# A new instruction order for the first 28 slices, on eight PSUM banks, with fillers that read a constant

## The chip, the core and the metric

The kernel runs on one core of one Trainium2 chip. The metric is the device time of one launch in microseconds (us). Times of single instructions come from one profiled execution of the kernel.

## The reference

A cross attention between a sequence and a small state, in both directions, feeds a gated feed-forward layer. For each of 8 batches and 8 heads, `x` has 512 rows and `state` has 32 rows, of 64 numbers each.

```python
scores  = scale * x @ state^T;   a  = softmax(scores);   xread = a @ state      # 512 rows per head
scores2 = scale * state @ x^T;   a2 = softmax(scores2);  sread = a2 @ x         # 32 rows per head
x = concat([xread, sread], axis=2).transpose(0, 2, 1, 3).reshape(B * S, H * D)  # (8 * 544) x 512
gate = maximum(x @ w_gate, 0);   val = x @ w_val         # d_model 512 -> d_ff 1536
return (gate * val) @ w_out                              # back to 512
```

## The kernel before

The kernel never forms `xread`. For a batch b it multiplies the state by the two weight matrices first (`U = state @ w`, per head), and then the normalised attention by `U`. All products are bf16 with float32 sums.

The work of one batch: transpose `x` on TensorE (`x_T`, `x_T2`, lines 169 to 186), or by a DMA in later batches; scores (`att_sc`, L200); exponential on ScalarE (`att_exp`, L207); row sums and reciprocals on VectorE (`att_sum`, L213 and L215); scaling (`att_scale`, L219) on VectorE or on GpSimd; transposing the attention (`att_T`, L235, copied out by `att_out`, L249). The state block is converted to bf16 (`state_conv`, L121 and L124), transposed (`state_T`, L129) and copied out (`state_out`, L133). `U` is made in units: `c_unit` covers a few columns of both weight matrices, `u_unit` covers 512 columns of one; both issue small tiled products in `u_mm` (L291), into two banks, one for each half of the heads, and are copied out by `c_out` (L311) and `u_out` (L301).

A slice (b, jf) is 128 of the 1536 hidden columns for the 512 rows of batch b: `gv` (L316) makes gate and value in four products of 512 columns into two banks, `relu` (L340) copies the gate out on ScalarE, and `mult` (L344) multiplies on VectorE. Three `o` steps of four products (`out_part`, L353) make an output tile of 128 rows, and `fin_x` (L361) copies it out and stores it. The state's own read (`sr_mm`, L264, with the bf16 copy `xa` of x that `x_pad`, L256, makes on GpSimd) is normalised on VectorE by a reciprocal and a scale (`sr_norm`, L271 and L273), which read the `sr` bank.

Every engine runs its instructions in the order in which the kernel issues them. The order has two parts. The first is a string, `program`: each word is a step. `gv.0.5@41` is slice (0, 5) with its two products in banks 4 and 1; `co.0.128.128.1.act` copies half 1 of a `c` unit out on ScalarE; `nx` is `att_scale`, `nr` is `att_sum`, `ex` is `att_exp`, `xc` converts x, `xo` copies its transposes out, `ao` is `att_out`, `sto` copies the state's transposes out, `stc` is `state_conv`, `xp` is `x_pad`, `sr` and `sn` are the state's read and its normalisation, `dw` loads a block of columns of one weight matrix, `dx`, `ds`, `do` and `df` are other loads. All of those loads are issued by GpSimd, in the order of the string. The string covers 28 slices: batches 0 and 1, and four slices of batch 2. The second part is a loop, which starts at slice (2, 4) and hands out banks by turns, beginning with banks 0 and 1:

```python
    def bank(name, kind="r"):
        if given:
            n = given.pop(0)
        ...
            n = turn["r"] % 6 if kind == "r" else 6 + turn["o"] % 2
```

In the string of before, banks 0 to 5 hold everything but the output tiles, which use 6 and 7. Bank 7 is also the target of the fillers. A filler (`spin`, L432) is a product of 128x512 whose result nobody reads. It reads `warm`, a piece of a buffer that is filled much later and which VectorE sets to zero first (L396). There are 23 fillers, all among the first steps.

Of the kernel before, what the change touches and what calls it, by code (L numbers as in the profile page):

```python
# [9 lines left out]
BF16 = mybir.dt.bfloat16  # L10
# [6 lines left out]
def kernel(  # L17
# [9 lines left out]
    nc = tc.nc  # L27
# [42 lines left out]
    stT = const.tile([128, B, NJ, 64], BF16, name="stT")  # L70
    br = const.tile([128, NJ, B, Ns], BF16, name="br")
    hs_sb = const.tile([128, NF, B * Ns], BF16, name="hs_sb")
    warm = hs_sb.rearrange("p f n -> p (f n)")[:, 0:512]
    tiny = const.tile([128, 1], FP32, name="tiny")

    xf, xb, xT, e_sn, a_sn, ANS, U, hsb, sr_sb = {}, {}, {}, {}, {}, {}, {}, {}, {}
# [316 lines left out]


    ctx.enter_context(tc.manual_schedule())
    nc.vector.memset(warm, 0.0)  # L396
    xf[0] = xin.tile([128, H, NC, D], FP32, name="xf", tag="xf")
    for eng, j in ((nc.sync, 0), (nc.scalar, None), (nc.scalar, 1)):
        if j is None:
# [28 lines left out]
    warm_ps = psum.tile([128, 512], FP32, name="warm_ps", tag="b7")  # L428

    def spin(n, cols=512):  # L430
        for i in range(n):
            nc.tensor.matmul(warm_ps[:, 0:cols], warm[:, 0:128], warm[:, 0:cols], start=True, stop=True)  # L432

    steps = {"spin": spin, "stc": state_conv, "stT": state_T, "sto": state_out, "xc": x_conv_pair, "xT": x_T, "xT2": x_T2, "xo2": x_out2, "on": lambda: nc.gpsimd.memset(xa[:, :, :, D:D + 1], 1.0), "dw": w_load, "dx": x_load, "ds": lambda: state_dma(nc.gpsimd, 2, B), "do": wo_dma,
             "df": lambda b: x_dma(b, (nc.gpsimd,)), "xo": x_out,
             "sc": att_sc, "ex": att_exp, "nr": att_sum, "nx": att_scale, "aT2": att_T2, "ao2": att_out2, "aT": att_T, "ao": att_out,
             "c": c_unit, "co": c_out, "u": u_unit, "uo": u_out, "gv": gv, "re": relu, "mu": mult, "o": out_part,
             "of": fin_x, "xn": x_next, "xp": x_pad, "sr": sr_mm, "sn": sr_norm}  # L440
    program = """
    dx.1.0.2 dx.1.1.2 stc.0.0.act stc.0.1.dve spin.7 stT.0@0 xc.0.0.dve dw.0.0.128 sto.0.act dw.1.0.128 on xc.0.1.dve
    spin.3 xT.0.1@1 dw.0.128.128 xT.0.0@2 xo.0.1.dve xo.0.0.act dw.1.128.128 spin.3 sc.0.0@3 dw.0.256.256 ex.0.0
    spin.1 xT.0.2@4 xT.0.3@5 xo.0.2.dve dw.1.256.256 xo.0.3.act nr.0.0 spin.3 sc.0.1@0 dw.0.512.256 xT2.1.0@1 ex.0.1
    nx.0.0 xo2.1.0.act nr.0.1 dw.1.512.256 spin.2 xT2.1.1@2 xo2.1.1.act sc.1.0@3 dw.0.768.256 nx.0.1 ex.1.0
    dw.1.768.256 spin.2 c.1.0.128@45 c.0.0.128@01 co.1.0.128.0.dve aT.0.1@2 co.0.0.128.0.act aT.0.0@3 co.1.0.128.1.dve
    co.0.0.128.1.act dw.0.1024.256 sc.1.1@4 ao.0.1.dve ao.0.0.act nr.1.0 ex.1.1 dw.1.1024.256 spin.2 c.0.128.128@05
    gv.0.0@12 co.0.128.128.1.act nr.1.1 co.0.128.128.0.act nx.1.0.pool re.0.0 gv.0.1@34 mu.0.0 re.0.1 nx.1.1.pool
    c.1.128.128@50 mu.0.1 co.1.128.128.1.act c.0.256.256@12 co.1.128.128.0.act c.1.256.256@30 dw.0.1280.256
    co.0.256.256.0.dve co.0.256.256.1.act aT.1.1@5 aT.1.0@4 co.1.256.256.0.act co.1.256.256.1.dve dw.1.1280.256  # L450
    gv.0.3@21 ao.1.1.act ao.1.0.dve dx.2.0.1 re.0.3 gv.0.2@30 mu.0.3 ds re.0.2 c.1.512.256@54 mu.0.2 gv.1.2@21
    co.1.512.256.1.act co.1.512.256.0.act do.0.6 c.0.512.256@30 re.1.2 gv.1.5@45 co.0.512.256.0.dve xp.1
    co.0.512.256.1.act mu.1.2 re.1.5 gv.1.3@23 mu.1.5 re.1.3 gv.1.1@04 do.6.12 mu.1.3 re.1.1 c.1.768.256@15 xp.0
    mu.1.1 gv.1.4@23 co.1.768.256.0.act co.1.768.256.1.act c.0.768.256@04 re.1.4 gv.1.0@15 co.0.768.256.0.dve
    co.0.768.256.1.act df.3 mu.1.4 re.1.0 gv.1.6@20 mu.1.0 re.1.6 gv.0.4@41 mu.1.6 re.0.4 gv.0.6@35 mu.0.4 re.0.6
    gv.1.7@20 mu.0.6 re.1.7 c.0.1024.256@41 c.0.1280.256@35 mu.1.7 co.0.1024.256.0.act xT2.2.0@2 stc.1.0.pool
    co.0.1024.256.1.act co.0.1280.256.1.dve xT2.2.1@0 stc.1.1.pool co.0.1280.256.0.act xo2.2.0.dve gv.0.5@41
    stc.3.0.pool stc.3.1.pool xo2.2.1.dve re.0.5 stc.2.1.pool gv.0.10@53 stc.2.0.pool mu.0.5 re.0.10 stT.1@2 gv.0.9@40
    mu.0.10 sto.1.act re.0.9 sc.2.1@1 gv.0.8@52 ex.2.1 mu.0.9 re.0.8 nr.2.1 gv.0.11@34 re.0.11 mu.0.8 gv.0.7@10
    nx.2.1.pool mu.0.11 re.0.7 sc.2.0@5 o.0.0@6 mu.0.7 ex.2.0 nr.2.0 c.1.1280.256@32 c.1.1024.256@14  # L460
    co.1.1280.256.1.act u.2.1.1024@50 o.0.1 co.1.1024.256.0.dve co.1.1024.256.1.act nx.2.0.pool uo.2.1.1024.1.dve
    uo.2.1.1024.0.act o.0.2 co.1.1280.256.0.act u.2.0.0@21 xn.3 of.0.0.dve u.2.1.0@45 uo.2.0.0.1.act u.2.1.512@03
    uo.2.1.0.0.dve o.0.3@7 uo.2.1.0.1.act uo.2.0.0.0.dve uo.2.1.512.0.act aT.2.0@1 aT.2.1@4 uo.2.1.512.1.dve
    ao.2.0.act o.0.4 ao.2.1.act o.0.5 gv.2.1@50 of.0.1.act re.2.1 gv.1.10@23 mu.2.1 re.1.10 gv.1.11@14 mu.1.10 re.1.11
    gv.2.3@50 mu.1.11 re.2.3 gv.2.2@23 mu.2.3 re.2.2 u.2.0.1024@14 u.2.0.512@50 mu.2.2 uo.2.0.1024.1.act sr.0@2
    o.0.6@6 uo.2.0.512.1.act uo.2.0.512.0.dve sn.0 gv.1.9@34 uo.2.0.1024.0.dve re.1.9 gv.1.8@05 mu.1.9 re.1.8
    gv.2.0@21 mu.1.8 re.2.0 o.0.7 mu.2.0 o.0.8 o.0.9@7 of.0.2.dve sr.1@3 sn.1 xp.2 xp.3
    """
    for word in program.split():
        word, _, banks = word.partition("@")  # L470
# [107 lines left out]
```

The softmax here doesn't subtract the row's maximum and nothing guards it: scores larger than these inputs give would overflow.

## Time and profile before

| | us |
|---|---|
| median of 4 runs | 225.6 |
| the 4 runs | 224.38, 225.58, 225.62, 225.64 |
| the profiled execution, whole | 225.11 |
| its span, first to last instruction | 223.3 |
| TensorE busy in it | 215.6 (97%) |
| first slice starts in it | 14.22 |
| the loop's first slice, (2, 4), starts in it | 56.72 |

The span is what the trace covers, so positions in the trace count from its first instruction, and 1.8 us of the profiled execution lie around it. A timeline line gives start, length, engine, source line, output and inputs, shapes and count; in square brackets stands the idle time of the engine before it and what ended that. "PE" is TensorE's products, "PEld" its weight loads.

The loads that GpSimd issues land one after the other. In this execution: the rest of batch 0 at 6.62 us, batch 1 at 8.46 and 9.77, the weight blocks from 10.49 to 26.64, batch 2 at 29.28, the rest of the state at 30.29, the two halves of the output weights at 34.0 and 37.83, and batch 3 at 40.74.

### The profile page before, as it was taken

The page shows a single profiled execution, that of the slowest core. Times are in us where ns is not written, and L with a number is a line of the kernel's source. Part 1 is how long each engine was busy: PE and PEld are TensorE (multiplying, and loading weights), DVE is VectorE, ACT ScalarE, POOL GpSimd, SP SyncE. Part 2 cuts the span into 40 slices and gives each one's busy share as a digit, 9 for nine tenths or more (in the row PEclk, how much of TensorE's full clock was granted, in tenths as well). Part 3 has the DMA queues.
Part 4 walks back from the last instruction along what each step waited for, and adds up shares of the span by engine and source line. Part 5 has one row for each costly group of instructions (what it writes and reads, how often), then busy time and mean ns, then how long its engine had stood idle before and what let it go on. Part 6 is the DMA issues. An engine that isn't in the chain of part 4 may idle for free.

```text
span 223.3 us, 4840 instructions
## 1 busy us (share of the span) xinstructions
PE 215.6 (97%) x1937; PEld 106.5 (48%) x1967; DVE 128.5 (58%) x226; ACT 124.8 (56%) x236; POOL 53.3 (24%) x58
## 2 busy tenths in 40 slices
PE   7999999999999999999999999999999999999994
PEld 3544455444544444444444444445444445666543
DVE  3587888666595648664877468646875433222100
ACT  4599877874467645675566456645655444222221
POOL 8889756503301525006000700000000000000000
PEclk9999999999999999999999999999999999999999
DMA  7999999160147671781159113511311111111132
GB/s 153 180 195 196 207 233 285 41 169 3 47 101 231 117 262 56 165 253 51 48 128 277 56 57 92 100 50 47 94 50 47 48 47 50 48 68 73 52 94 94
DMA packets 37799, 25.48 MB, mean 114 GB/s; under 512 B 18864, under 2 KB 33200, under 8 KB 37776
## 3 DMA queue, kind: packets, MB, share of 16 engines
q1 hardware_dynamic: 24912, 16.85, 26.6%
q0 software_dynamic: 11968, 7.47, 21.6%
q10 hardware_dynamic: 896, 0.85, 1.4%
q8 instruction: 15, 0.25, 0.4%
q14 instruction: 8, 0.07, 0.1%
HBM read 18.35 MB, written 8.91 MB: 122 GB/s over the span
## 4 chain that ended last, share of the span: by engine, by line
PE 95%; issue 2%; ACT 1%; DVE 0%; DVEq 0%
PE o_ps L353 38%; PE gv_ps L316 37%; PE gv_ps L333 5%; PE up L291 4%; PE warm_ps L432 3%; PE sc_ps L200 2%; PE upc L291 1%; PE sr_ps L264 1%; PE o_ps L379 1%; ACT U L311 1%; PE aT_ps L235 1%; PE xT_ps L186 1%; PE stT_ps L129 0%; ACT xT L189 0%; PE xT_ps L169 0%
## 5 line engine op out<-in xcount | busy, mean ns | idle before, releaser
L316 PE MATMUL gv_ps<-ans,U 128*128 128x512 bf16 x373 | 93.9, 379 | 0.5
L353 PE MATMUL o_ps<-wo_sb,h_sb 128*128 128x512 bf16 x357 | 91.6, 379 | 2.1 <-issue 1.9
L344 DVE TENSOR_TENSOR h_sb<-gv_ps,g_sb 128x512 bf16<-128x512 f32 x96 | 65.4, 689 | 43.8 <-ACT g_sb L340 42.6
L340 ACT ACTIVATE g_sb<-gv_ps 128x512 bf16<-128x512 f32 (+1 forms) x108 | 62.7, 580 | 49.2 <-PE gv_ps L316 34.5
L316 PEld LDWEIGHTS <-U 128*128 128x128 bf16 x384 | 35.8, 98 | 40.4 <-issue 0.6
L353 PEld LDWEIGHTS <-h_sb 128*128 128x128 bf16 x372 | 35.2, 98 | 39.8 <-issue 1.7
L361 ACT COPY o_sb<-o_ps 128x512 f32<-128x512 f32 x29 | 17.1, 590 | 16.5 <-PE o_ps L353 16.5
L301 ACT CAST U<-up 128x512 bf16<-128x512 f32 x36 | 18.9, 594 | 11.4 <-PE up L291 11.4
L301 DVE CAST U<-up 128x512 bf16<-128x512 f32 x36 | 22.8, 684 | 2.2 <-PE up L291 1.9
L142 POOL CAST xb<-xf 128x1024 bf16<-128x1024 f32 x10 | 10.6, 1088 | 52.6 <-DMA xf<-in_x_dram 45.7
L256 POOL COPY xa<-xb 128x2048 bf16<-128x2048 bf16 (+1 forms) x9 | 15.3, 1709 | 12.5 <-issue 7.6
L213 DVE TENSOR_REDUCE cs<-e_sn 128x16 f32<-128x512 bf16 x16 | 10.9, 684 | 7.9 <-ACT e_sn L207 7.9
L344 DVE TENSOR_TENSOR hs_sb<-gv_ps,g_sb 128x256 bf16<-128x256 f32 x12 | 5.1, 425 | 15.3 <-PE gv_ps L333 10.5
L207 ACT ACTIVATE e_sn<-sc_ps 128x512 bf16<-128x512 f32 x16 | 9.6, 599 | 5.6 <-PE sc_ps L200 5.5
L291 PEld LDWEIGHTS <-stT 64*32 64x32 bf16 x512 | 5.7, 89 | 11.3 <-issue 10.1
L311 ACT CAST U<-upc 128x512 bf16<-128x512 f32 (+1 forms) x20 | 9.5, 533 | 1.4 <-PE upc L291 1.3
L432 PE MATMUL warm_ps<-hs_sb 128*128 128x512 bf16 x20 | 7.8, 504 | 1.4 <-DVE hs_sb L396 1.2
L219 DVE TENSOR_TENSOR a_sn<-e_sn,rc 128x512 bf16<-128x512 bf16 x12 | 8.3, 692 | 0.6
L200 PEld LDWEIGHTS <-xT 128*128 128x128 bf16 x128 | 5.7, 98 | 3.8 <-ACT xT L177 0.7
L291 PE MATMUL up<-wg_sb,stT 64*32 64x512 bf16 x144 | 7.4, 382 | 0.0
L333 PE MATMUL gv_ps<-br,wg_sb 128*128 128x256 bf16 x48 | 7.2, 273 | 0.1
L333 PE MATMUL gv_ps<-br,wv_sb 128*128 128x256 bf16 x48 | 7.2, 273 | 0.0
(64 smaller groups left out, 130.3 us busy)
## 6 DMA issues: line engine op xcount, KB each, us to landing
out_dram<-o_sb SPq DMA_DIRECT2D x31, 256.0 KB, 2.3
xf<-in_x_dram SPq DMA_DIRECT2D x4, 1024.0 KB, 6.3
wo_sb<-in_moe_w_out_dram POOLq DMA_DIRECT2D x2, 768.0 KB, 14.4
wg_sb<-in_moe_w_gate_dram POOLq DMA_DIRECT2D x5, 256.0 KB, 8.6
wv_sb<-in_moe_w_val_dram POOLq DMA_DIRECT2D x5, 256.0 KB, 9.2
xf<-in_x_dram POOLq DMA_DIRECT2D x1, 1024.0 KB, 15.1
xb<-in_x_dram POOLq DMA_DIRECT2D x3, 256.0 KB, 6.1
xb<-in_x_dram POOLq DMA_DIRECT2D x1, 512.0 KB, 11.1
```

Source lines behind the costliest of these rows:

```text
L213: nc.vector.reduce_sum(out=cs, in_=e_v, axis=AX.X)
L256: nc.gpsimd.tensor_copy(out=v[:, hs:hs + src.shape[1]], in_=src)
L291: nc.tensor.matmul(dst[parity][32 * j:32 * j + 32], stT[r:r + 64, b, j, 32 * parity:32 * parity + 32], wsb[r:r + 64, j, lo:lo + n], start= ...
L301: copy[eng](out=U[b][:, w, kc, lo:lo + 512], in_=held["u", b, w, lo][kc])
L311: copy[eng](out=U[b][:, :, kc, lo:lo + n], in_=held["c", b, lo][kc])
L316: nc.tensor.matmul(ps[w], U[b][:, w, kc, f0:f0 + 128], ANS[b][:, kc].rearrange("p c t -> p (c t)"), start=(kc == 0), stop=(kc == NK - 1))
L333: nc.tensor.matmul(ps[w][:, 0:nt], wsb[:, j, f0:f0 + 128], br[:, j].rearrange("p b n -> p (b n)"), start=(j == 0), stop=(j == NJ - 1))
L340: nc.scalar.activation(out=g_sb[:, 0:n], in_=ps[0][:, 0:n], func=AF.Relu)
L344: nc.vector.tensor_tensor(out=dst, in0=ps[1][:, 0:n], in1=held["g", b, jf][:, 0:n], op=ALU.mult)
L353: nc.tensor.matmul(held["o", b, tsub], src[:, jf, tsub * 128:(tsub + 1) * 128], wo_sb[:, jf], start=(jf == 0), stop=(jf == NF - 1))
L361: copy[eng](out=o_sb, in_=held["o", b, tsub])
L432: nc.tensor.matmul(warm_ps[:, 0:cols], warm[:, 0:128], warm[:, 0:cols], start=True, stop=True)
```

## The change

The order of the string is new, and so are the banks in it. Banks 6 and 7 now also hold slices, units and scores. There are 16 fillers in place of 23; they read a built-in constant of ones, one column wide, spread over 128 and 512 columns, and the memset is gone. Some steps change their engine: the scaling `nx` of batches 1 and 2 moves from GpSimd to VectorE, the first half conversion `xc.0.0` from VectorE to ScalarE, and several copies change between ScalarE and VectorE. Units of `U` for neighbouring columns stand next to each other more often, and the state reads `sr.0` and `sr.1` stand together at the end, in banks 2 and 0. The loop is unchanged.

```diff
-    warm = hs_sb.rearrange("p f n -> p (f n)")[:, 0:512]
...
-    nc.vector.memset(warm, 0.0)
+    one = nc.const_aps.tensor(1.0, (128, 1), BF16)
...
-            nc.tensor.matmul(warm_ps[:, 0:cols], warm[:, 0:128], warm[:, 0:cols], start=True, stop=True)
+            nc.tensor.matmul(warm_ps[:, 0:cols], one.to_broadcast([128, 128]), one.to_broadcast([128, cols]), start=True, stop=True)
...
-    dx.1.0.2 dx.1.1.2 stc.0.0.act stc.0.1.dve spin.7 stT.0@0 xc.0.0.dve dw.0.0.128 sto.0.act dw.1.0.128 on xc.0.1.dve
-    spin.3 xT.0.1@1 dw.0.128.128 xT.0.0@2 xo.0.1.dve xo.0.0.act dw.1.128.128 spin.3 sc.0.0@3 dw.0.256.256 ex.0.0
-    spin.1 xT.0.2@4 xT.0.3@5 xo.0.2.dve dw.1.256.256 xo.0.3.act nr.0.0 spin.3 sc.0.1@0 dw.0.512.256 xT2.1.0@1 ex.0.1
...
-    gv.0.0@12 co.0.128.128.1.act nr.1.1 co.0.128.128.0.act nx.1.0.pool re.0.0 gv.0.1@34 mu.0.0 re.0.1 nx.1.1.pool
-    c.1.128.128@50 mu.0.1 co.1.128.128.1.act c.0.256.256@12 co.1.128.128.0.act c.1.256.256@30 dw.0.1280.256
...
-    o.0.6@6 uo.2.0.512.1.act uo.2.0.512.0.act sn.0 gv.1.9@34 uo.2.0.1024.0.dve re.1.9 gv.1.8@05 mu.1.9 re.1.8
-    gv.2.0@21 mu.1.8 re.2.0 o.0.7 mu.2.0 o.0.8 o.0.9@7 of.0.2.dve sr.1@3 sn.1 xp.2 xp.3
+    dx.1.0.2 dx.1.1.2 stc.0.0.act stc.0.1.dve xc.0.0.act dw.0.0.128 spin.7 stT.0@0 xT.0.0@1 xc.0.1.dve dw.1.0.128 on
+    sto.0.dve xT.0.1@2 xo.0.0.dve dw.0.128.128 xo.0.1.act dw.1.128.128 dw.0.256.256 spin.4 xT.0.3@3 dw.1.256.256
+    xT.0.2@4 xo.0.3.dve sc.0.0@5 xo.0.2.act ex.0.0 sc.0.1@6 dw.0.512.256 xT2.1.0@0 ex.0.1 nr.0.0 xo2.1.0.act
...
+    co.0.0.128.0.dve aT.0.0@2 co.0.0.128.1.act ao.0.1.dve dw.1.1024.256 ao.0.0.act spin.1 c.1.128.128@43 nr.1.1
+    c.0.128.128@56 co.1.128.128.1.act gv.0.0@01 co.0.128.128.0.act nr.1.0 co.0.128.128.1.act dw.0.1280.256 re.0.0
+    gv.0.1@23 co.1.128.128.0.act nx.1.1 re.0.1 nx.1.0 dw.1.1280.256 c.0.256.256@57 c.1.256.256@60 co.0.256.256.1.act
+    co.0.256.256.0.dve aT.1.0@4 aT.1.1@2 co.1.256.256.0.act ao.1.0.dve gv.0.2@75 dx.2.0.1 ao.1.1.dve
...
+    c.1.1024.256@57 xo2.2.0.act stc.3.0.pool gv.1.10@10 co.1.768.256.0.dve stc.2.0.pool co.1.768.256.1.dve
+    co.1.1024.256.1.act stc.2.1.pool stT.1@4 gv.1.11@23 stc.3.1.pool re.1.10 sto.1.dve co.1.1024.256.0.act mu.1.10
...
+    mu.2.0 gv.2.2@34 of.0.1.act re.2.2 gv.1.6@20 mu.2.2 re.1.6 o.0.6@6 mu.1.6 o.0.7 o.0.8 gv.2.1@15 of.0.2.dve re.2.1
+    gv.2.3@34 mu.2.1 re.2.3 o.0.9@7 mu.2.3 sr.0@2 sr.1@0 sn.0 sn.1 xp.2 xp.3
```

## The prediction

> **What bounds the kernel now.** I read the page's shares first, then the chain that ended last. TensorE is busy for 97% of the span and carries 95% of the chain, the other engines 58% at most:
>
> ```profile
> PE 215.6 (97%) x1937; PEld 106.5 (48%) x1967; DVE 128.5 (58%) x226; ACT 124.8 (56%) x236; POOL 53.3 (24%) x58
> ...
> PE 95%; issue 2%; ACT 1%; DVE 0%; DVEq 0%
> ```
>
> A busy share hides waits, because a matmul's end is modelled. So I went on to the chain in order of time:
>
> ```profile
> 11.44 1.01 ACT xT L189
> ...
> 45.04 4.32 PE gv_ps L316 x20
> ```
>
> The last line is 20 products of 512 columns in 4.32 us, 0.216 us each. That is the price of a product in a dense stretch, so a `gv` slice or an `o` step (four products) costs 0.864. By start times, TensorE is dense from the first `gv` (14.22 us) to the end: only the weight and U groups cost more than their products. Before 14.22 it runs fillers and waits on a chain of transposes, copies (the first line is one on ScalarE), exponentials and sums. The hand-written program ends where slice (2,4) of the loop begins, at 56.72 us; the 166.6 us from there to the end of the span have the same instructions in both kernels. So the question is when slice (2,4) starts.
>
> Two views give the clocks of that stretch. The timeline of TensorE's head:
>
> ```profile
> 1.18 3.17 PE L432 MATMUL warm_ps<-hs_sb 128*128 128x512 bf16 x7 [1.18 <-DVE hs_sb L396]
> ...
> 5.84 0.96 PE L169 MATMUL xT_ps<-id,xb 128*128 128x128 bf16 x8
> 6.64 0.81 PE L432 MATMUL warm_ps<-hs_sb 128*128 128x512 bf16 x3
> ```
>
> The first seven fillers start 0.427 apart, those from 6.64 on 0.216 apart; within the eight transposes the spacing falls from 0.107 to 0.056 at about 6.5 us. And the timeline around the end of the program and of GpSimd's state work:
>
> ```profile
> 30.38 5.43 POOL L124 TENSOR_SCALAR st_b<-st_f,odd 128x256 bf16<-128x256 f32 x6 [3.87 <-DMA st_f<-in_state_dram]
> ```
> ```profile
> 56.35 0.43 PE L264 MATMUL sr_ps<-xa,e_sn 128*32 128x65 bf16 x32
> ...
> 56.72 1.04 PE L316 MATMUL gv_ps<-ans,U 128*128 128x512 bf16 x3
> 56.85 0.17 DVE L271 RECIPROCAL rr<-sr_ps 128x2 f32<-128x2 f32 x1 [0.56 <-PE sr_ps L264]
> ...
> 57.06 0.29 DVE L273 TENSOR_TENSOR sn<-sr_ps,rr 128x128 bf16<-128x128 f32 x1
> ```
>
> GpSimd waits 3.87 us for the state load, then needs 0.91 us for each of six conversions. TensorE goes on to `gv` straight after `sr`, while VectorE still reads the `sr` bank until 57.35.
>
> **Fillers.** 16 instead of 23. The memset (0.27 us, L396) and TensorE's wait for it go, so the first filler starts at about 0.8 instead of 1.18. This gains nothing: the seven end at 3.8, and `stT.0` needs `st_b`, whose VectorE half ends at 4.01 as before (the state block lands at 3.4). I cost the new operand at nothing: it is a product of the same 128x512 shape, and a few tenths more would still end before 4.1.
>
> **Head.** I followed each engine by hand with the rows' durations (ScalarE: copies and exponentials of 512 0.6, of 1024 1.01; VectorE: sum and reciprocal 0.96, scale 0.69, copies of 512 0.42 to 0.69). `xc.0.0` moves to ScalarE (done 4.55), so the first transposes start at 4.65 instead of 5.84. The rest of x0 lands at 6.62 and is transposed next, so both scores can run early: exp 0.0 ends at 8.7 (8.52 before), exp 0.1 at 9.3 (10.36 before). The halves of x1 land at 8.46 and 9.77 on the same queue; the second half's transposes start at 9.9 instead of 10.76, and its copy ends at 11.6 instead of 12.45. ScalarE then has exp 1.0, a cast, exp 1.1, a cast and `ao.0.0`, which ends at 13.7. `gv.0.0`: **13.76** against 14.22, 0.46 earlier.
>
> **Dense part, work.** Both have 28 `gv` and 10 `o` steps: 38 x 0.864 = 32.83. A `c` or `u` unit costs 0.217 and entering and leaving such a group about 0.22: one unit alone took 0.437 (19.47 to 19.90), two 0.653, three 0.866. Before has 17 units in 9 groups behind `gv.0.0`, one of them half wide, and one bank wait of 0.47 (at 16.47): 16 x 0.217 + 0.12 + 9 x 0.22 + 0.47 = 6.04. After has 16 units in 7 groups: 5.01. The two `sr` take 0.84 now; next to each other 0.71. The remaining transposes and scores are 2.7 in before and 2.64 in after (one batch's two half transposes lie between tiled units). The 42.50 from `gv.0.0` to (2,4) in before are these and 0.09 that I can't place; after comes to 41.28, if nothing waits. That alone would put (2,4) at 55.04.
>
> **Dense part, waits.** I checked each bank and each operand of the new order against the engine that frees it. Most have 0.1 us to spare or more. Four do not.
> First, `nx.1.*` moves from GpSimd to VectorE (two scales of 0.69), and `co.0.256.256.0` is queued behind them: sums from 13.2, scales to 16.5, cast to 17.15. `gv.0.2` needs it; TensorE would be there at 16.6. The wv columns of that unit also land only at 15.93. Wait: 0.5.
> Second, `stT.1` needs the first two state conversions. The state load lands at 30.29 behind the same loads on the same queue, so the second conversion ends at 32.22; TensorE arrives at about 32.0 (33.34 before, where this wait didn't show). Wait: 0.3 to 0.4. This ties the schedule to the DMA: what the head wins beyond it is lost, what the head loses up to 0.3 costs nothing.
> Third, `ao.2.*` and the U casts queue on VectorE behind `nx.2.1` and the output copy: 0.15.
> Fourth, the seam. `sr.1` moves from bank 3 to bank 0, and the loop's next slice (2,4) takes banks 0 and 1; the order of the built program has its weight load wait for VectorE, without such a wait before. `sn.0` stands ahead of `sn.1` on VectorE. From the start S of `sr.0`: its last product at S+0.24, reciprocal 0.26 later, scale to S+1.0, then reciprocal and scale of `sr.1` to S+1.47, TensorE at S+1.6; without the wait S+0.61. Price: 1.0, with `o`, scores and the whole loop queued behind it on TensorE. The bounds are 0.75 (the second pair alone after `sr.1`: 0.26 + 0.21 + 0.29 after its last product) and 1.1.
>
> **Sum.** 55.04 + 0.5 + 0.35 + 0.15 + 0.98 = 57.0, against 56.72: **0.3 us later**. Gains of about 1.7 (0.46 head, 1.03 groups and units, 0.2 the rest) meet new waits of 2.0. The span becomes 223.6. The profiled execution took 225.11 for a span of 223.3, 1.8 around it; the median of the four runs is 225.6 (224.38 to 225.64), so the forecast is 225.9.
>
> **A clock that stays half longer** (rival, slower). Row: in before, TensorE was occupied almost without a gap from 1.18, and full speed came at about 6.5. After drops the three fillers from 4.56 to 5.84, has gaps at 3.8 to 4.15 and around 4.6, and puts transposes there instead. Full speed came 5.3 after the first filler; as long after the fillers begin again at 5.63 would be 10.9. Then the fillers and transposes up to there cost twice (0.427, 0.107): the scores end 0.9 later, `gv.0.0` is at 14.65 to 14.8, the slack at `stT.1` takes up 0.4 of it: 0.5 to 0.6 more, 226.5. If it comes only once the slices run, two of them take 1.73 instead of 0.86 on top, less what the waits absorb: 1.2 to 1.6 more, up to 227.5. It decides from the point where TensorE's head is late by more than the 0.4. For it: the gaps. Against it: the change to full speed in before fell among eight transposes, and later runs of 16 keep the 0.055 spacing.
> The Trainium skill speaks against this part of the change: "TensorE: Matmul & The Clock Gate" (Part 1) says the full clock follows a sustained busy window of about 3.4 us, and Part 4 says that transposes do not count as busy in the same way. The row at 6.5 us agrees with a window but can't separate transposes from fillers. By that rule alone the estimate would be one window more, full speed near 10 us, and a total of 226.4.
>
> **The waits are shorter** (rival, faster). If the loads run ahead of before's landings because GpSimd no longer computes between its DMA issues (2.05 us of scales at 14.7), and the second wait goes, and the seam costs 0.75, (2,4) starts at 56.4; with the first wait gone too, 55.9: 224.8. Only if the seam wait also went, at 55.2, would it be 224.1. Against it: the DMA engines moved 186 GB/s on average up to 45 us, without an empty slice until the loads end, so the landing times are set by bytes.
>
> **The change does not do what it says**: the instruction order shows 16 fillers and no wait for a memset, so only the seam's bank could be read wrongly; that is the faster case.
>
> **Chances.** About what a measurement of this kernel can tell from no change is 0.5%, 1.1 us: 224.5 to 226.7. My forecast has 0.47, of which 0.08 falls above 226.7 by queues on ScalarE and VectorE that run a little later than I walked. The slow clock has 0.35: 0.26 above 226.7, 0.09 below. The shorter waits have 0.18: 0.10 under 224.5. Faster 0.10, same 0.56, slower 0.34. The range runs from 224.7 to 227.2: it takes in the lower cases with two waits gone and the slow clock to its middle.
>
> **What would show it.** Right: (2,4) starts near 57 us; `stT.1` waits for GpSimd's `st_b` at about 32.3; the first `gv` is near 13.8; a hole of some 1 us on TensorE before (2,4), ended by VectorE's `sn`. Wrong: fillers or transposes at half speed past 6.6 us, `gv.0.0` after 14.2, a `gv` slice in the first 30 us that takes over 0.9, or no hole at the seam.

## The result, and the profile after

| | us |
|---|---|
| changed kernel, median of 39 runs | 226.04 (225.09 to 227.53) |
| kernel before, median of 58 runs beside them | 225.13 (224.38 to 225.89) |
| ratio, with its 95% interval | 1.0043 [1.0035, 1.0052] |
| profiled execution of the changed kernel, whole / span | 227.0 / 225.2 |
| its first slice | 15.02 (before 14.22) |
| its slice (2, 4) | 58.60 (before 56.72) |

The changed kernel is slower by 0.9 us; the forecast was 0.3 us. The profiled execution is itself 1.0 us above the median of its kernel, while that of before was at its median, so 1.9 us between the two traces are not the change alone. One word of the diff under "The change" is to be read differently: in the removed line that begins with `o.0.6@6`, the kernel before has `uo.2.0.512.0.dve`, not `.act`.

The shares of the page and its chain, in the changed kernel:

```profile
PE 214.1 (95%) x1931; PEld 106.3 (47%) x1960; DVE 130.9 (58%) x232; ACT 123.3 (55%) x233; POOL 49.0 (22%) x54
...
PE 87%; DMA 7%; DVE 2%; issue 2%; ACT 0%; POOL 0%; POOLq 0%; DVEq 0%
```

TensorE is busy 1.5 us less than before, and its share of the chain fell from 95% to 87%. A DMA share of 7% is new: 7% of 225.2 us is 16 us, and the chain in order of time shows where they lie (start, length, what):

```profile
1.43 6.36 DMA xb<-in_x_dram
7.79 0.28 issue
8.08 9.87 DMA wv_sb<-in_moe_w_val_dram
17.95 0.04 issue
17.99 0.52 PE upc L290 x24
```

So up to 18 us loads set the pace: first the rest of batch 0, which landed at 7.79 (6.62 in before), then the value columns of the first unit of 256 columns, at 17.95 (15.93 in before). The timeline of TensorE's head shows the two waits:

```profile
4.14 0.59 PE L128 MATMUL stT_ps<-id,st_b 128*128 128x128 bf16 x4 [0.23 <-DVE st_b L123]
...
5.58 1.50 PE L431 MATMUL warm_ps<-const-bfloat16-1.0 128*128 128x512 bf16 x4
7.83 0.64 PE L172 MATMUL xT_ps<-id,xb 128*64 128x128 bf16 x16 [0.75 <-DMA xb<-in_x_dram]
...
16.84 0.30 PE L290 MATMUL upc<-wg_sb,stT 64*32 64x256 bf16 x8
17.99 0.30 PE L290 MATMUL upc<-wv_sb,stT 64*32 64x256 bf16 x8 [0.85 <-DMA wv_sb<-in_moe_w_val_dram]
```

The four fillers from 5.58 take 1.50 us together. The first two start 0.43 before the next one, the third only 0.26: full speed came at 6.53 us, where before had it at 6.56.

Around the state's conversion on GpSimd (weight loads of TensorE, then GpSimd):

```profile
32.40 2.73 POOL L123 TENSOR_SCALAR st_b<-st_f,odd 128x256 bf16<-128x256 f32 x3 [3.80 <-DMA st_f<-in_state_dram]
```
```profile
34.28 0.23 PEld L128 LDWEIGHTS <-st_b 128*128 128x128 bf16 x4 [0.71 <-POOL st_b L123]
```

The state landed at 32.30 (30.29 in before). GpSimd needs 0.91 us for each conversion, and the weight load of `stT.1` waits 0.71 for the second of them. And the seam:

```profile
57.14 0.70 PE L263 MATMUL sr_ps<-xa,e_sn 128*32 128x65 bf16 x64
57.64 0.17 DVE L270 RECIPROCAL rr<-sr_ps 128x2 f32<-128x2 f32 x1 [0.37 <-PE sr_ps L263]
57.84 0.29 DVE L272 TENSOR_TENSOR sn<-sr_ps,rr 128x128 bf16<-128x128 f32 x1
58.05 0.16 DVE L270 RECIPROCAL rr<-sr_ps 128x2 f32<-128x2 f32 x1
58.25 0.29 DVE L272 TENSOR_TENSOR sn<-sr_ps,rr 128x128 bf16<-128x128 f32 x1
58.59 1.04 PE L315 MATMUL gv_ps<-ans,U 128*128 128x512 bf16 x3 [0.75 <-DVE sn L272]
```

The 64 products of both `sr` now stand together. The last begins at 57.65, VectorE works through two pairs of reciprocal and scale until 58.54, and only then does slice (2, 4) start: 0.94 us after that product, where before had 0.13. From (2, 4) to the end both traces take 166.6 us (225.19 - 58.595; 223.31 - 56.72).

### The profile page after: what moved, and what is told of

Same layout as the page of the kernel before. It is cut to its first block, busy times and chain, and to the rows that moved or that the text cites. A ratio compares the mean times of both kernels' runs of the same rounds, so it can differ in the third digit from the quotient of the medians.

```text
span 225.2 us, 4814 instructions
## 1 busy us (share of the span) xinstructions
PE 214.1 (95%) x1931; PEld 106.3 (47%) x1960; DVE 130.9 (58%) x232; ACT 123.3 (55%) x233; POOL 49.0 (22%) x54
## 4 chain that ended last, share of the span: by engine, by line
PE 87%; DMA 7%; DVE 2%; issue 2%; ACT 0%; POOL 0%; POOLq 0%; DVEq 0%
PE o_ps L352 38%; PE gv_ps L315 35%; PE gv_ps L332 5%; DMA wv_sb<-in_moe_w_val_dram 4%; PE up L290 4%; DMA xb<-in_x_dram 3%; PE sc_ps L199 1%; PE o_ps L378 1%; PE sr_ps L263 1%; DVE U L310 1%; PE upc L290 1%; PE aT_ps L234 0%; PE stT_ps L128 0%; DVE h_sb L343 0%; ACT g_sb L339 0%
## 5 line engine op out<-in xcount | busy, mean ns | idle before, releaser
L343 DVE TENSOR_TENSOR h_sb<-gv_ps,g_sb 128x512 bf16<-128x512 f32 x96 | 64.7, 688 | 42.3 <-ACT g_sb L339 41.1
L300 DVE CAST U<-up 128x512 bf16<-128x512 f32 x35 | 22.1, 683 | 2.2 <-PE up L290 1.9
L218 DVE TENSOR_TENSOR a_sn<-e_sn,rc 128x512 bf16<-128x512 bf16 x16 | 11.4, 726 | 0.3
L310 ACT CAST U<-upc 128x512 bf16<-128x512 f32 (+1 forms) x18 | 8.8, 544 | 2.0 <-PE upc L290 2.0
L310 DVE CAST U<-upc 128x512 bf16<-128x512 f32 (+1 forms) x10 | 6.1, 631 | 1.7 <-PE upc L290 1.7
```

The lines of the kernel that those rows point to most:

```text
L218: {"dve": nc.vector, "pool": nc.gpsimd}[eng].tensor_tensor(out=by_pair(a_sn[b], jp).rearrange("p r (j n) -> p r j n", n=Ns), in0=e_v, in1= ...
L300: copy[eng](out=U[b][:, w, kc, lo:lo + 512], in_=held["u", b, w, lo][kc])
L310: copy[eng](out=U[b][:, :, kc, lo:lo + n], in_=held["c", b, lo][kc])
L343: nc.vector.tensor_tensor(out=dst, in0=ps[1][:, 0:n], in1=held["g", b, jf][:, 0:n], op=ALU.mult)
```

## The experiments

My theory was that two things set the start of (2, 4) in the changed kernel: the seam, a fixed price of some 0.8 us, and the landing of the state, to which `stT.1` ties all that follows. The rivals were a TensorE clock that stays half longer because of the new head, and the new fillers themselves. The runs below serve four questions. Ratios are to runs of before on the same chip in the same session; they are not quotients of the medians beside them, and can differ from these by up to 0.15%.

**The seam, taken out and put in.** In the changed kernel `sr.1` goes back to bank 3; in before it goes to bank 0.

```diff
 (in the changed kernel)
-    gv.2.3@34 mu.2.1 re.2.3 o.0.9@7 mu.2.3 sr.0@2 sr.1@0 sn.0 sn.1 xp.2 xp.3
+    gv.2.3@34 mu.2.1 re.2.3 o.0.9@7 mu.2.3 sr.0@2 sr.1@3 sn.0 sn.1 xp.2 xp.3
 (in before)
-    gv.2.0@21 mu.1.8 re.2.0 o.0.7 mu.2.0 o.0.8 o.0.9@7 of.0.2.dve sr.1@3 sn.1 xp.2 xp.3
+    gv.2.0@21 mu.1.8 re.2.0 o.0.7 mu.2.0 o.0.8 o.0.9@7 of.0.2.dve sr.1@0 sn.1 xp.2 xp.3
```

> The changed kernel with sr.1 in bank 3 instead of bank 0, so that slice (2,4) doesn't wait for VectorE's normalisation. Theory seam: the hole of 0.94 us between the last sr product and slice (2,4) shrinks to 0.13, and the time falls by 0.8 us, to about 225.2. Rival: a wait that only moves, for slice (2,5) takes banks 2 and 3 next, or VectorE's queue is late anyway; then the time falls by under 0.3.

> The kernel before with sr.1 in bank 0 instead of bank 3, the seam's bank alone put into the old order. Theory seam: VectorE needs 0.26 + 0.20 + 0.29 after the last sr product and TensorE a further 0.1, in place of 0.13, so slice (2,4) starts 0.7 us later and the time rises by 0.7 (0.3%). Less than in the changed kernel, for sn.0 doesn't stand ahead of sn.1 here. Rival: no change, if the loop catches up.

> The changed kernel once more, for a second trace. In its first trace the loads of GpSimd landed later than in before: the rest of x0 at 7.8 us (6.6), the value columns of the 256-column unit at 18.0 (15.9), the state at 32.3 (30.3). Theory chance: the landings differ from execution to execution, this trace lies near before's landings, and slice (2,4) starts near 57.3 us, the median near 226.0. Rival fillers: fillers that read a constant, or the missing memset, slow the early loads every time; then the rest of x0 lands at 7.5 or later again and slice (2,4) starts at 58 or later.

Measured: the changed kernel again 225.65 us, 1.0019 [1.0000, 1.0038]; with `sr.1` in bank 3 224.75, 0.9992 [0.9979, 1.0004]; before with `sr.1` in bank 0 225.91, 1.0034 [1.0018, 1.0049]; before itself 225.26. The timeline of the changed kernel with bank 3:

```profile
56.79 0.71 PE L263 MATMUL sr_ps<-xa,e_sn 128*32 128x65 bf16 x64
57.43 1.04 PE L315 MATMUL gv_ps<-ans,U 128*128 128x512 bf16 x4
...
57.89 0.29 DVE L272 TENSOR_TENSOR sn<-sr_ps,rr 128x128 bf16<-128x128 f32 x1
```

and of before with bank 0:

```profile
57.18 0.29 DVE L273 TENSOR_TENSOR sn<-sr_ps,rr 128x128 bf16<-128x128 f32 x1
57.53 1.04 PE L316 MATMUL gv_ps<-ans,U 128*128 128x512 bf16 x4 [0.62 <-DVE sn L273]
```

With bank 3 the slice starts while VectorE still scales, and `stT.1` to (2, 4) takes 23.48 us instead of 24.31: 0.83 less. With bank 0 in before the slice waits for VectorE's `sn`, 0.81 after the last product (0.13 without it), and the median rises by 0.65 us. In time, bank 3 gains 0.90 us by the medians and 0.6 by the ratios (1.0019 against 0.9992). The price is shown in both directions, in the trace and in the time. The seam alone is thus about as large as what the change cost in all (0.9 and 0.4 us in the two sessions), so the rest of the change must come to little in sum.

**The landings.** The same kernels were run for other traces, and both kernels got one more load of 128x4x128 numbers on GpSimd's queue (256 KB read, into columns of a buffer that is filled much later), ahead of the first weights: all later loads come later by its time.

```diff
+    extra = hs_sb[:, 4:6].rearrange("p f (a n) -> p (f a) n", n=128)
+    def x_extra():
+        nc.gpsimd.dma_start(out=extra, in_=moe_w_out.rearrange("(f p) m -> p f m", p=128)[:, 0:NJ, 0:128])
...
-    dx.1.0.2 dx.1.1.2 stc.0.0.act
+    dx.1.0.2 dx.1.1.2 dd stc.0.0.act
```

> The changed kernel with one load more, of 128x512 numbers (256 KB read) into a buffer that is not used yet, between batch 1 and the first weights on GpSimd's queue: every later load lands about 0.7 us later. Theory landing: the new order has no slack against the weights and the state, so the time rises by the same 0.6 to 0.7 us. Rival queues: VectorE and ScalarE set the pace of the first slices, and the time rises by under 0.2.

> The kernel before with the same extra load. Theory landing: TensorE comes to the value columns of the 256-column unit about 0.3 us after they land and to the state's transposes about 1 us after, so the old order absorbs part: the time rises by 0.2 to 0.4 us. If it rises by as much as the changed kernel, the old order was bound by the same landings.

> The kernel before once more, for a second trace of its landings: rest of x0 at 6.6 us, value columns at 15.9 and state at 30.3 in the first. Theory chance: landings that differ by a microsecond between executions of the same kernel. Rival fillers: the same landings again, within 0.2 us.

Measured: the changed kernel with the load 226.15 us, 1.0056 [1.0035, 1.0076]; before with it 225.52, 1.0015 [1.0003, 1.0028]; before again 225.17, 0.9997 [0.9986, 1.0008], beside 225.19 of before. The load cost before 0.33 us and the changed kernel 0.3 to 0.8, by which of its two ratios one starts from; the direction agrees with the tie, the size is not separated from 0.33 by these intervals. The second traces fell between their expectations: the changed kernel's rest of batch 0 landed 0.5 us earlier than in its first and its state 1.0 earlier, before's 0.6 and 0.2 later. The positions in the traces say more. From the traces of the runs with the state converted as in the two kernels, in us:

| kernel | full clock | second half of batch 1 landed | `gv.0.0` | state landed | `stT.1`, after that landing | (2, 4), after `stT.1` | whole |
|---|---|---|---|---|---|---|---|
| before | 6.56 | 9.77 | 14.22 | 30.29 | 3.05 | 23.38 | 225.11 |
| before, again | 5.00 | 10.15 | 13.65 | 30.49 | 2.60 | 23.37 | 224.81 |
| before, new fillers | 6.45 | 10.36 | 14.21 | 30.36 | 2.97 | 23.37 | 225.06 |
| before, `sr.1` in bank 0 | 4.53 | 10.85 | 14.35 | 30.85 | 2.62 | 24.06 | 225.89 |
| before, extra load | 6.93 | 11.28 | 15.35 | 32.01 | 2.52 | 23.38 | 226.27 |
| after | 6.53 | 11.21 | 15.02 | 32.30 | 1.99 | 24.31 | 227.00 |
| after, again | 4.18 | 10.20 | 14.01 | 31.29 | 1.99 | 24.31 | 225.88 |
| after, old fillers | 6.08 | 10.62 | 14.43 | 31.00 | 1.99 | 24.31 | 225.58 |
| after, extra load | 3.58 | 10.76 | 15.10 | 32.58 | 1.98 | 24.31 | 227.59 |
| after, `sr.1` in bank 3 | 11.48 | 11.53 | 16.09 | 31.54 | 2.40 | 23.48 | 225.70 |
| the same, old fillers | 6.51 | 10.58 | 14.39 | 31.32 | 1.98 | 23.49 | 225.07 |

In five of the six traces of the new order `stT.1` starts 1.98 to 1.99 us after the state lands, however early or late that is, and (2, 4) follows after a constant. The sixth is the one whose clock stayed half until 11.48. In before the distance is 2.5 to 3.1 and varies: there (2, 4) keeps 42.5 us from `gv.0.0`, once 42.8 (42.50, 42.81, 42.49, 42.55; 43.18 with the seam put in). So in these traces before's time follows its head, and the new order's time follows the landing of the state:

`(2, 4) = landing + 1.99 + 24.31` with the seam, `landing + 1.99 + 23.49` without it.

Two conversions account for 1.83 of the 1.99. The timeline of the changed kernel's second trace shows the same (GpSimd, then TensorE):

```profile
31.38 5.43 POOL L123 TENSOR_SCALAR st_b<-st_f,odd 128x256 bf16<-128x256 f32 x6 [4.89 <-DMA st_f<-in_state_dram]
```
```profile
33.27 0.40 PE L128 MATMUL stT_ps<-id,st_b 128*128 128x128 bf16 x4 [0.34 <-POOL st_b L123]
```

Put before's own landing, 30.29, into the first formula: (2, 4) at 56.59, 0.13 before its 56.72. So by the formula, what made the changed kernel's trace 1.88 us later than before's at (2, 4) was that its loads landed late; at equal landings the seam's 0.8 and the gains of the new order cancel.

**The fillers.** The two fillers were exchanged, first in each kernel alone:

```diff
-    warm = hs_sb.rearrange("p f n -> p (f n)")[:, 0:512]
...
-    nc.vector.memset(warm, 0.0)
+    one = nc.const_aps.tensor(1.0, (128, 1), BF16)
...
-            nc.tensor.matmul(warm_ps[:, 0:cols], warm[:, 0:128], warm[:, 0:cols], start=True, stop=True)
+            nc.tensor.matmul(warm_ps[:, 0:cols], one.to_broadcast([128, 128]), one.to_broadcast([128, cols]), start=True, stop=True)
```

This is the edit in before; the same lines backwards give the new order with the old fillers.

> The kernel before with the new fillers alone: they read the constant of ones, and the memset is gone; order, banks and number of fillers as before. Theory chance: no difference (within 0.2 us), the first filler at 0.76 instead of 1.18, loads land as in before (rest of x0 near 6.6). Rival fillers: the early loads land about 1 us later (rest of x0 at 7.5 or later), and the time rises by 0.3 to 1.0.

> The new order and banks with the old fillers, which read a buffer of zeros that VectorE sets first (16 of them). Theory chance: the same time as the changed kernel (within 0.2 us, near 226.0). Rival fillers: the loads land as early as in before, slice (2,4) starts near 57.0, and the time is near 225.4.

Measured: before with the new fillers 225.63 us, 1.0018 [1.0002, 1.0033]; the new order with the old ones 225.30, 1.0007 [0.9994, 1.0021], against 1.0043 and 1.0019 with the new ones. Both would say that the new fillers cost 0.3 to 0.8 us. But in the trace of before with the new fillers (2, 4) starts at 56.70 (56.72 with the old), and the next runs went against it.

**Both parts together, and the tie cut.** First the new order with the old fillers and `sr.1` in bank 3 (both diffs above). Then, with bank 3, the second state conversion of `stT.1` moved to ScalarE, so that GpSimd has only one to make before TensorE needs them; with the new fillers, with the old ones, and with the new ones and an eighth filler in the first group, so that TensorE does not stand before the first transposes.

```diff
-    co.1.1280.256.0.dve xT2.2.0@3 stc.1.0.pool co.0.1280.256.0.act c.1.768.256@26 xo2.2.1.dve stc.1.1.pool
+    co.1.1280.256.0.dve xT2.2.0@3 stc.1.0.pool co.0.1280.256.0.act c.1.768.256@26 xo2.2.1.dve
...
-    co.1.1024.256.1.act stc.2.1.pool stT.1@4
+    co.1.1024.256.1.act stc.1.1.act stc.2.1.pool stT.1@4
...   (the third kernel alone)
-    spin.7 stT.0@0
+    spin.8 stT.0@0
```

> The new order with the old fillers and with sr.1 in bank 3. Theory seam: 0.8 us below the new order with old fillers, near 224.5. On the fillers: the changed order with sr.1 in bank 3 and new fillers had a ratio of 0.9992; if the new fillers cost 0.3 us or more, this one lies at 0.998 or below, if they cost nothing, at 0.999 again.

> The changed kernel with sr.1 in bank 3 and the second half of the state conversion, stc.1.1, on ScalarE (behind co.1.1024.256.1) instead of GpSimd. In four traces of the new order the state's transposes started 1.98 to 1.99 us after the state landed, 1.84 of it two conversions one after the other on GpSimd, and slice (2,4) 24.3 us later. Theory landing: the transposes start about 1.1 us after the landing unless TensorE is later, so the time falls by 0.3 to 0.8 us below sr.1 in bank 3 alone (ratio near 0.997). Rival queues: VectorE's casts of the units before hold the transposes at the same place, no gain.

> The same with the old fillers. Best of the versions if the new fillers cost something: ratio 0.996 or below. If they cost nothing, equal to the one before within 0.1%.

> The same with new fillers and eight instead of seven ahead of the state's first transposes. The new fillers start 0.41 us earlier and so leave a gap of 0.4 us before those transposes. Theory gap: it is the gap in TensorE's activity that costs something, because full speed then comes late in more executions (at 11.5 us in one trace); the eighth filler brings the old fillers' time back. Rival constant: reading the constant itself costs; then eight equals seven.

| kernel | median | ratio to before |
|---|---|---|
| new order, old fillers, bank 3 | 225.12 | 0.9982 [0.9965, 0.9999] |
| bank 3, split, new fillers | 225.07 | 0.9989 [0.9979, 0.9999] |
| bank 3, split, old fillers | 225.42 | 1.0004 [0.9990, 1.0019] |
| bank 3, split, eight new fillers | 225.34 | 0.9999 [0.9988, 1.0011] |

The split did not bring the 0.3 to 0.8 us expected of it (0.9989 against 0.9992 without it). It did not cut the wait, it moved it. The timelines of the first split kernel (GpSimd, then ScalarE, then TensorE):

```profile
30.73 4.53 POOL L123 TENSOR_SCALAR st_b<-st_f,odd 128x256 bf16<-128x256 f32 x5 [4.08 <-DMA st_f<-in_state_dram]
```
```profile
31.20 1.05 ACT L188 COPY xT<-xT_ps 128x1024 bf16<-128x1024 bf16 x1
32.10 0.63 ACT L310 CAST U<-upc 128x512 bf16<-128x512 f32 x1
32.58 0.55 ACT L120 ACTIVATE st_b<-st_f,odd 128x256 bf16<-128x256 f32 x1
```
```profile
33.27 0.38 PE L128 MATMUL stT_ps<-id,st_b 128*128 128x128 bf16 x4 [0.84 <-ACT st_b L120]
```

The state landed at 30.64, but on ScalarE the conversion stands behind a copy and a cast and starts only at 32.58. `stT.1` comes 2.63 after the landing (2.68 and 2.76 in the other two), later than the 1.99 with both on GpSimd.

The fillers have now been exchanged in four pairs. New against old is 0.2% slower in before; 0.1 to 0.4% slower in the new order; 0.1% slower in the new order with bank 3 (0.9992 against 0.9982, intervals overlapping); and 0.15% faster with the split. The pair in before alone is clear of noise, narrowly (its interval begins at 1.0002). With the signs mixed, no effect of theirs is established, and none is excluded below some 0.3%. The eighth filler brought nothing (0.9999 against 0.9989 with seven), so the gap ahead of the first transposes is not shown to cost anything.

The five versions with `sr.1` in bank 3 lie between 0.9982 and 1.0004, three of them just below before: 0.9982, 0.9989 and 0.9992. Two of the intervals end at 0.9999, so a gain over before is at most 0.35% and may be nothing. All five are faster than the changed kernel's 1.0043; with the 1.0019 [1.0000, 1.0038] of its second session three of the five intervals overlap.

## Why the prediction was right, and where its steps were not

The direction and two mechanisms stand, the seam and the tie to the state's load. That the time agrees so well, 225.9 forecast against 226.04, is luck: the median of before that it started from, 225.6, was 0.5 above the 225.13 measured beside the changed kernel, and the change was forecast as 0.3 us and measured as 0.9 (0.4 in the second session), so two errors nearly cancel. Of the prediction's own four signs of being right, two came, the hole ended by `sn` and the wait of `stT.1` for GpSimd (at 34.28, not 32.3). The other two did not: (2, 4) came at 58.60 and 57.59 in the changed kernel's two traces, not near 57, and the first `gv` at 15.02 and 14.01, the first of them past the 14.2 that was named as a sign of being wrong. By steps:

**The seam** was the right mechanism with nearly the right price: 0.98 forecast, bounds 0.75 and 1.1, and the hole grew by 0.81 in the first trace, 0.83 without against with. From the start S of `sr.0` the walk had the first scale done at S+1.0, the second at S+1.47, TensorE at S+1.6; the lines above give S+0.99, S+1.40 and S+1.45. Half of the 0.15 too much is the second pair, half TensorE's restart.

**The head**, `gv.0.0` at 13.76, was 0.46 earlier than 14.22 only against one trace. The new head ends 3.81 us after the second half of batch 1 lands in four of the six traces above; the other two are the one with the extra load and the one with the late full speed (9.77 + 3.81 = 13.58 at the landing of before's trace; the forecast was 13.76, so the walk was right to 0.2). But before's own head reaches 3.50 where full speed came at 5.0 or earlier, and needs 3.85 and 4.45 where it came at 6.45 and 6.56 (the trace with the extra load, 4.07, also waited 0.52 for weight columns). At equal landings and with an early full speed the old head would be 0.31 ahead of the new one. So the traces suggest that the 0.46 belonged to one execution's clock; no run tested this by itself.

**The dense work**, 41.28, can be read from the one trace of the new order where neither the state's landing nor the seam stood in the way (`sr.1` in bank 3): 57.43 - 16.09 = 41.34, small waits included. The price of groups and units holds.

**The first wait** was named as VectorE's queue before `gv.0.2`, 0.5. That was the wrong one of the two given: TensorE waited for the value columns, 0.85 where they landed at 17.95, some 0.1 in the second trace of the changed kernel (16.04). In the trace with `sr.1` in bank 3, where TensorE itself was late, it did not wait for them at all. VectorE's cast did end a wait before `gv.0.2`, but of about 0.16: in these three traces the slice starts 0.65 to 0.67 after the transposes ahead of it, in before 0.50. 41.34 leaves no room for 0.5.

**The second wait** is where the sum failed. The mechanism, "this ties the schedule to the DMA", is shown by five traces. (In the first of them VectorE's cast into `U` ended at the same moment, 34.28, so the product's own record names that; in the second the cast was done at 33.11, and GpSimd alone is left.) The value was not: the step took over 30.29 from before's trace, with the reason that the landing times are set by bytes. They are not set by bytes alone. Over the traces without an extra load, the same load lands between 30.29 and 30.85 in before's order and between 30.06 and 32.30 in the new one. In the changed kernel's profiled execution that term alone is 2.0 us. The terms behind it were 0.4 too large: the forecast had 2.06 from the landing to `stT.1`, measured 1.99, and 24.65 from there to (2, 4), measured 24.31. In the 24.65 were the seam, 0.15 too large, and the third wait, 0.15, which doesn't show: in the two traces with `sr.1` in bank 3 and both conversions on GpSimd, no product of TensorE waits between 34.5 us and (2, 4). With both, 57.0 + 2.0 - 0.4 is the 58.6 of the trace. At before's landing the change would have come to -0.13 us.

The forecast's claim for this wait, that what the head loses up to 0.3 costs nothing, can be checked in the trace with the late full speed: the head came 0.75 later than 11.53 + 3.81, and `stT.1` came 0.41 later than the landing allows; 0.34 was absorbed.

**The slow clock** exists. The timeline of TensorE in the trace with `sr.1` in bank 3:

```profile
6.89 1.91 PE L431 MATMUL warm_ps<-const-bfloat16-1.0 128*128 128x512 bf16 x4
...
11.02 0.84 PE L185 MATMUL xT_ps<-id,xb 128*64 128x128 bf16 x16
...
12.33 0.64 PE L185 MATMUL xT_ps<-id,xb 128*64 128x128 bf16 x16
```

The fillers from 6.89 still start 0.43 apart, and the transposes from 11.02, which start in pairs, go from 0.106 to 0.056 a pair at 11.48 us, near the 10.9 that the rival named. That execution took 225.70, 0.95 above the median of its kernel, but its loads were late too. The late full speed is no explanation of the changed kernel's trace, where full speed came at 6.53. In 13 of the 14 traces it came between 3.6 and 6.9 us. How many of the unprofiled runs have it is not known; the highest single time of the second session, 227.31 in twelve, may or may not be one. The Trainium skill, "TensorE: Matmul & The Clock Gate" (Part 1), says that the window is free-running, and that the onset therefore differs from run to run by 0.5 us either way. The traces agree that it differs, and the spread is wider here: 3.6 to 6.9 us, once 11.48. Part 4 of that page, by which transposes do not count as busy, gave an estimate of full speed near 10 us; the changed kernel's two traces, at 6.53 and 4.18, did not follow it, the first of them with little but transposes and gaps from 4.1 to 5.6 us.

**Left open.** Why the loads land later in the new order, and whether they do on average. Eight traces of it without an extra load have a mean landing of the state of 31.14 us, four of before 30.50; the ranges overlap. The difference of 0.64, with the -0.13 of the formula, would give 0.5, between the 0.4 and the 0.9 measured, but profiled executions are too few to carry that. The view of the DMA's rates shows one place. Up to 34 us, in 40 slices, first in the changed kernel, then in before:

```profile
GB/s 0 0 145 351 301 130 124 119 159 167 180 169 180 179 189 193 197 214 183 193 196 196 195 197 196 208 188 195 195 196 195 199 213 328 269 218 222 213 208 214
```
```profile
GB/s 0 0 125 358 312 123 149 175 186 198 182 178 178 183 197 213 185 193 194 198 196 193 199 195 202 196 193 195 199 195 198 199 281 327 246 205 219 199 205 206
```

Between 5 and 8.5 us (the seventh to tenth number) the changed kernel moves 119 to 167 GB/s, before 149 to 198; after 11 us the rates are alike. The rest of batch 0 was under way in this stretch, and landed 1.17 us later. But the rest of batch 0 landed at 7.74 and 7.76 in two traces of before's order too, so the order does not own it. Single loads of 256 KB, mostly some 1.33 us apart, came 2.4 to 2.8 us after the one ahead of them in four traces of the new order, and at most 1.9 in those of before. What delays them I did not find. Whether it would go away with the scales back on GpSimd was not tried.

## What to carry to other kernels

A schedule that follows another engine's queue and one that follows a load answer to different things: before trusting a time from one trace, take two executions and see which event keeps a constant distance to the work behind it. When a reorder makes TensorE reach a load sooner, the gain ends where the load lands, and its landing has to be carried into the sum as a range, not as the value of one trace. And where an order written by hand ends, look at the banks that the next part takes first: a single bank number cost 0.8 us here, about as much as all that the reorder lost.

## What the runs showed of the hardware that was not expected

- The same load in the same queue, behind the same bytes, landed up to 2.2 us apart over the traces of the new order's versions (the state: 30.06 to 32.30 us) and 1.0 us apart in two executions of the changed kernel (32.30 and 31.29). Single loads of 256 KB came as late as 2.4 to 2.8 us after the one ahead of them, in place of 1.33.
- TensorE's full speed came anywhere from 3.58 to 6.93 us, and once at 11.48, from the span's start.
- A filler that reads a stretched constant costs what one from a buffer does: 0.43 us at the half clock (seven in 3.15 us, against 3.17) and 0.216 at the full one.
